# Polysketch attention and a GELU layer on one core: batch 0's key products and numerators in 128x64 tiles over block-diagonal operands

## The chip, the cores and the metric

The kernel runs on one core of one Trainium2 chip. Its time is the device time of one execution in microseconds (us), and the figure compared is the median over several runs. One execution was also taken by the hardware profiler; durations of single steps come from it.

## The reference

Queries, keys and values have the shape (batch 4, heads 4, tokens 1088, 32). S1 and S2 are two 8 x 32 sketches. All is fp32.

```python
def phi(x):                       # 64 features of a token and head
    a = np.einsum('rd,bhsd->bhsr', S1, x)
    b = np.einsum('rd,bhsd->bhsr', S2, x)
    return np.einsum('bhsi,bhsj->bhsij', a, b).reshape(*x.shape[:-1], r * r)
q_p, k_p = (phi(q), phi(k))
kv = np.einsum('bhsf,bhsd->bhfd', k_p, v)
z = np.sum(k_p, axis=2)
num = np.einsum('bhsf,bhfd->bhsd', q_p, kv)
den = np.einsum('bhsf,bhf->bhs', q_p, z)[..., None] + 1e-06
x = (num / den)                   # heads side by side: 4352 tokens x 128
h = x @ w_in                      # 128 x 2048
out = (0.5 * h * (1.0 + erf(h * inv_sqrt2))) @ w_out   # 2048 x 128
```

## The kernel before

The tokens are cut into chunks of 512 (two to a batch, n = 0 to 7, and a last one of the 64 left over in each batch). For each chunk TensorE makes 16 hidden tiles of 128 x 512 (`hidden`, L735), ScalarE applies GELU to each (L742), and TensorE multiplies with w_out (`project`, L872; from the ninth hidden tile on with fewer products out of sums of blocks, L821, whose sums GpSimd makes at L786 to L789). Two PSUM banks are shared by the hidden tiles (pool hps), two by the outputs (ops), and four, in two pairs, by everything else (wps). The weights arrive as 64-bit numbers and are turned into fp32 by some six instructions a piece (`Rounding`, L263 to L305), dealt out over VectorE, ScalarE and GpSimd.

Every engine runs its instructions in the order of the text: the last lines of the kernel chain each instruction to the one before it on its engine. So the order around the change is the order of the lines, and a wait of one instruction holds up all that stand behind it.

Only batch 0 takes part in the change. It goes through these steps, all in the first 20 us:

- `keep_busy` (L904) multiplies zeros until the first keys have landed.
- `key_turn` and `key_turn_apart` transpose the keys (L341, L369): in `kT[r]` the rows are 4 tokens x 32, the columns token groups of heads r and r + 2.
- `key_products` (L390) multiplies them with `S12`, a block-diagonal matrix of the two sketches for four tokens (128 rows, 4 x 16 columns). It works in 64 x 64 tiles of TensorE: the upper and the lower 64 rows, which are two tokens each, go to different banks, and each uses the 32 columns of S12 that belong to its two tokens.
- `key_features` multiplies the two sketches into 64 features a token (ScalarE L403, L406; VectorE L407; GpSimd L404), and `kv_first` (L434, with L440 for the left-over tokens) sums features times values, widened by a column of ones (`v_aug`), in tiles of 128 x 64. The sum, the numerators' matrix and in column 33 the denominators' vector, is copied to `kz[0]` (L941): rows 0 to 63 for one head of a pair, rows 64 to 127 for the other.
- `expand_products` (L557) makes the query features of a chunk, with 64 rows for each head of a pair, in 32 x 64 tiles; ScalarE (L564) and VectorE (L569) finish them as `qp[n]`.
- `numerators_by_token` (L670) multiplies 64 tokens' features of one head with the 33 columns of `kz[0]`. The heads of a pair are the upper and lower half of the rows, so it too runs in 64 x 64 tiles, into one bank for each half.
- `divide` adds 1e-6 to the denominators (L687; for the second half of chunk 0 ScalarE does it, L701), inverts them (L688) and multiplies (L693) into `x_tok`. `turn_half` and `turn_half_apart` transpose that (L716, L708) and copy it to `xT` (L717, L710), which `first_hidden` (L751) and `hidden` read.

Chunk 0 passes through the last two steps in two halves of two tokens each, with banks of their own; chunk 1 in one piece, while the first hidden tiles are made. Later, `repeat_first_z` copies parts of `kz[0]` for the one left-over chunk.

Of the kernel before, what the change touches and what calls it, by code (L numbers as in the profile page):

```python
# [8 lines left out]
FP = mybir.dt.float32  # L9
U32 = mybir.dt.uint32  # L10
AX = mybir.AluOpType
# [5 lines left out]
def kernel(  # L17
# [29 lines left out]
    JC = 4  # L47
# [26 lines left out]
    def halves(banks):  # L74
        return [banks[:, i] for i in range(2)]

    def hidden_bank():
        return hps.tile([128, CW], FP, name="h_ps")

    def out_bank():  # L80
        return ops.tile([128, CW], FP, name="o_ps")
# [149 lines left out]
    kz = [big.tile([128, 128], FP, name=f"kz{b}") for b in range(B)]  # L231

    kz_first = big.tile([128, 128], FP, name="kz_first")

    ones = big.tile([128, D], FP, name="ones")

# [1 line left out]
    pool.memset(v_rem_aug[0], 0.0)  # L238
    pool.memset(v_rem_aug[0][:REM], 1.0)
    dve.memset(ones, 1.0)  # L240

    v_aug = [att.tile([128, NP, J, 2 * D], FP, name="sums") for r in range(2)]
    for t in v_aug:
# [137 lines left out]
        return dict(out=out, in0=a[:, :, :, None].broadcast_to([128, n, R, R]),  # L381
                    in1=b[:, :, None, :].broadcast_to([128, n, R, R]))

    def key_products(r, banks, col=0):

        for i in range(2 * NCH):
            for c in range(2):
                for t in range(2):
                    at = i * 128 + c * 64
                    pe.matmul(banks[t][c * 64:(c + 1) * 64, col + i * 32:col + (i + 1) * 32],  # L390
                              lhsT=kT[r][t * 64:(t + 1) * 64, at:at + 64],
                              rhs=S12[t * 64:(t + 1) * 64, 2 * t:2 * t + 2].rearrange("p h r -> p (h r)"),
                              start=True, stop=True)

    def key_features(b, r, banks, by_pool=()):
        key_products(r, banks)
# [28 lines left out]
    def flat(features):  # L425
        return features.rearrange("p i j -> p (i j)")

    def kv_first(ps, r, tokens=range(J)):

        for i in tokens:  # L430

            ch, t, one = i // 4, i // 2 % 2, i % 2
            for c in range(NP):
                pe.matmul(ps[c * F:(c + 1) * F, r * 2 * D:r * 2 * D + C], lhsT=flat(k_p[0, r][:, t, c * 4 + ch * 2 + one]),  # L434
                          rhs=v_aug[r][:, c, i, :C], start=(r == 0 and i == 0), stop=False, skip_group_check=True)

    def kv_first_rem(ps):
# [67 lines left out]

    def repeat_first_z():

        of = kz[0].rearrange("f (r x) -> f r x", r=2)
        to = kz_first.rearrange("f (c r d) -> f c r d", c=NP, r=2)
        for c in range(NP):  # L510
            act.copy(out=to[:F, c], in_=of[c * F:(c + 1) * F, :, 0:D])
        zs = att.tile([128, 2, D], FP, name="z_cols")
        pool.tensor_copy(out=zs, in_=of[:, :, D:C].broadcast_to([128, 2, D]))
        held["zs"] = zs

    def turn_first_kv():
# [142 lines left out]

    x_tok = {}  # L660

    def numerators_by_token(n, banks, tokens):

        for at, i in enumerate(tokens):
            for r in range(2):
                for half in range(2):
                    for c in range(NP):
                        rows, col, tok = slice(c * F, (c + 1) * F), (at * 2 + r) * C, i * 128 + half * 64
                        v_at = r * 2 * D
                        pe.matmul(banks[c][half * 64:(half + 1) * 64, col:col + C], lhsT=qp[n][rows, r, tok:tok + 64],  # L670
                                  rhs=kz[0][rows, v_at:v_at + C], start=True, stop=True)

    def x_half(n, i):
        x_tok[n, i] = att.tile([128, 2, H, D], FP, name=f"x_tok{i}", bufs=1)
        return x_tok[n, i]

    def divide(n, banks, tokens, by_head_pair, den=None):

        g = len(tokens) * 2
        given = den is not None  # L680
        if not given:
            den = att.tile([128, NP, JC * 2], FP, name="den_tok")[:, :, :g]
        parts = [slice(c, c + 1) for c in range(NP)] if by_head_pair else [slice(0, NP)]
        nd = [(banks[c.start][:, None] if by_head_pair else banks)[:, :, :g * C].rearrange("p b (g c) -> p b g c", c=C)
              for c in parts]
        for c, x in zip(parts, nd) if not given else ():
            dve.tensor_scalar(out=den[:, c], in0=x[:, :, :, D], scalar1=1e-6, scalar2=None, op0=AX.add)  # L687
        dve.reciprocal(out=den, in_=den)  # L688
        for i in range(len(tokens) // 2):
            to = x_half(n, tokens[0] // 2 + i).rearrange("p j (c r) d -> p c j r d", c=NP)  # L690
            for c, x in zip(parts, nd):
                for b in range(c.stop - c.start):
                    dve.tensor_mul(out=to[:, c.start + b], in0=x[:, b, i * 4:i * 4 + 4, 0:D].rearrange("p (j r) d -> p j r d", r=2),  # L693
                                   in1=den[:, c.start + b, i * 4:i * 4 + 4].rearrange("p (j r) -> p j r", r=2)[:, :, :, None]
                                   .broadcast_to([128, 2, 2, D]))

    def denominators(banks):

        den = att.tile([128, NP, JC * 2], FP, name="den_tok")[:, :, :JC]
        for c, ps in enumerate(banks):  # L700
            act.activation(out=den[:, c], in_=ps[:, :JC * C].rearrange("p (g c) -> p g c", c=C)[:, :, D], func=ACT.Copy, bias=1e-6)  # L701
        return den

    def turn_half_apart(n, i, banks):
# [196 lines left out]
    def keep_busy(n, ps, cols=256):  # L901
        for i in range(n):
            noughts = [nc.const_aps.tensor(0.0, [128, m], FP) for m in (128, cols)]
            pe.matmul(ps[:, CW - cols:], lhsT=noughts[0], rhs=noughts[1], start=True, stop=True)  # L904

    bank = work_bank()
    keep_busy(3, bank)
    keep_busy(1, bank, 192)
    r = Rounding(SR)
    r.fields(by_dve=True)  # L910
    r.mantissas()
# [13 lines left out]
    for i in range(2):  # L925
        query_features(0, i)
    kv_bank = out_bank()
    kv_first(kv_bank, 0, (0, 1, 4, 5))
    key_turn_rem(0, banks[1], by_act)
    kv_first(kv_bank, 0, (2, 3, 6, 7))  # L930
    key_features_rem(0, banks[1])
    kv_first(kv_bank, 1)
    kv_first_rem(kv_bank)
# [3 lines left out]
    w_in[0].exponents()  # L937
    late = []
    query_turn(1, lambda **a: late.append(a))
    kz_of, kv_of = (x.rearrange("f (r x) -> f r x", r=2)[:, :, :C] for x in (kz[0], kv_bank[:, :128]))  # L940
    act.copy(out=kz_of, in_=kv_of)  # L941
    w_in[0].mantissas()
    w_in[0].signs()
    w_in[0].product(pool)
# [3 lines left out]
    by_act(**late[0])  # L948
    w_in[1].low_words()
    parts = [range(2), range(2, JC)]  # L950
    nd = [[hidden_bank(), hidden_bank()], [out_bank(), out_bank()]]
    for banks, tokens in zip(nd, parts):
        numerators_by_token(0, banks, tokens)
    den = denominators(nd[1])
    expand_products(1)
    divide(0, nd[0], parts[0], by_head_pair=True)
    w_in[1].exponent_fields()
    w_in[1].exponents()
    divide(0, nd[1], parts[1], by_head_pair=True, den=den)
    turn_half(0, 0, hidden_bank(), by_act)  # L960
    w_in[1].mantissa_fields()
    turn_half_apart(0, 1, [out_bank(), out_bank()])
# [212 lines left out]
    for t in range(len(steps) + LAG):  # L1175
        if t < 4:

            hidden(0, t)
            if t == 1:
                w_out[0].low_words()  # L1180
                w_out[0].exponents()
                w_out[0].finish()
                w_out[1].fields()
            if t == 2:
                w_out[1].low_words()
            if t == 3:
                banks = work_banks()
                numerators_by_token(1, halves(banks), range(JC))
                w_out[1].mantissas(by_pool=True)
                w_out[1].exponents()  # L1190
                divide(1, banks, range(JC), by_head_pair=False)
                w_out[1].signs()
                w_out[1].product()
                project(0, 0)
                project(0, 1, cols=slice(0, 256))
                turn_half(1, 0, work_bank(), by_act)
                project(0, 1, cols=slice(256, 512))
                turn_half(1, 1, work_bank(), by_dve)
            continue
        if t == 4:  # L1200
            first_hidden(1, 0)
            for f, *a in products[t]:
                f(*a)
            first_hidden(1, 1)
        for n in drains[t]:
            drain(n)
        sooner = t == NMAIN * NF
        if sooner:
            for f, *a in products[t]:
                f(*a)  # L1210
        if t < len(steps):
            n, fi = steps[t]
            hidden(n, fi, by_halves=t >= 18 and (n < NMAIN or fi < 5))
        if t < len(steps) and steps[t][0] < NMAIN and steps[t][1] % NB == NB - 1:
            n, b = steps[t][0], steps[t][1] // NB
            if b >= first_block(n):
                token_sums(n, b)
        for f in slots[t]:
            f()
        for n in done[t]:  # L1220
            store(n)
        if t != 4 and not sooner:
            for f, *a in products[t]:
                f(*a)
# [41 lines left out]
```

## Time and profile before

| | |
|---|---|
| median of 3 runs | 259.53 us (259.43 to 259.59) |
| profiled execution, its own time | 259.29 us |
| its span, first to last instruction | 257.5 us |
| TensorE busy | 253.3 us (98%), 2333 instructions |
| VectorE, ScalarE, GpSimd busy | 151.7, 114.4, 164.1 us |
| key products L390 | 2 x 32 instructions, from 5.93 to 7.07 us |
| numerators L670 | 2 x 32 instructions from 11.74 us, 64 from 18.58 us |

The profile counts instructions: an fp32 product is two, each a load of weights (PEld) and a multiplication (PE). A row of the timeline gives start, duration, engine, line, operation, the tile written and those read, and the shape, "rows*columns" of the TensorE tile first. In brackets is the idle time of the engine before it and what ended it. Times of single instructions, where they are given to three digits, are records of the same trace.

### The profile page before, as it was taken

To read this page: it belongs to the slowest core of one execution; us is meant where nothing else is said; L and a number is where in the kernel's file an instruction comes from. 1 tells how busy PE (TensorE), PEld (TensorE's weight loads), DVE (VectorE), ACT (ScalarE), POOL (GpSimd) and SP (SyncE) were. 2 spreads that over 40 slices of the span, in tenths; PEclk is the share of its full clock that TensorE was granted. 3 is DMA by queue.
4 is the path that set the end of the run, shared out by engine and by line. 5 is a ranking of instruction groups with operands and counts; after the bars stand their busy time and mean duration, and the time that the engine had idled before them with its cause. 6 is when DMAs were issued, how large, how long until landed. Compare 5 with 4: busy or idle time off the path is not lost.

```text
span 257.5 us, 5763 instructions
## 1 busy us (share of the span) xinstructions
PE 253.3 (98%) x2333; PEld 135.0 (52%) x2333; DVE 151.7 (59%) x317; ACT 114.4 (44%) x221; POOL 164.1 (64%) x173
## 2 busy tenths in 40 slices
PE   8999999999999999999999999999999999999995
PEld 6856444355444545444444455455544444445794
DVE  3886879969698987580178976399307000700330
ACT  3685767433635333533335332523444334433442
POOL 3503016799968788587758775787758777877300
PEclk9999999999999999999999999999999999999999
DMA  6479848820000101101000002000200200020020
GB/s 208 136 221 368 179 105 210 224 47 10 3 0 13 30 1 23 20 12 31 3 0 3 0 10 36 1 1 3 41 3 7 37 0 1 7 36 0 3 41 20
DMA packets 29082, 13.48 MB, mean 52 GB/s; under 512 B 21888, under 2 KB 27264, under 8 KB 29056
## 3 DMA queue, kind: packets, MB, share of 16 engines
q1 hardware_dynamic: 28624, 12.79, 20.2%
q8 instruction: 18, 0.29, 0.5%
q10 hardware_dynamic: 432, 0.33, 0.4%
q14 instruction: 8, 0.07, 0.1%
HBM read 10.88 MB, written 2.23 MB: 51 GB/s over the span
## 4 chain that ended last, share of the span: by engine, by line
PE 98%; DVE 1%; issue 0%; ACT 0%; DVEq 0%
PE h_ps L735 45%; PE o_ps L821 33%; PE o_ps L872 5%; PE w_ps L869 3%; PE w_ps L445 1%; PE w_ps L592 1%; PE w_ps L904 1%; PE w_ps L647 1%; PE o_ps L434 1%; PE h_ps L751 1%; PE w_ps L989 1%; PE w_ps L557 0%; PE w_ps L670 0%; DVE x_tok L693 0%; PE h_ps L341 0%; PE w_ps L341 0%
## 5 line engine op out<-in xcount | busy, mean ns | idle before, releaser
L735 PE MATMUL h_ps<-xT,w_in 128*64 128x512 f32 (+3 forms) x514 | 136.8, 576 | 0.0
L742 ACT ACTIVATE block<-h_ps 128x512 f32<-128x512 f32 (+1 forms) x128 | 73.0, 571 | 117.3 <-PE h_ps L735 115.3
L735 PEld LDWEIGHTS h_ps<-xT,w_in 128*64 128x64 f32 (+1 forms) x514 | 41.7, 142 | 30.6 <-issue 11.9
L821 PE MATMUL o_ps<-block,w_out 128*64 128x256 f32 x224 | 57.5, 379 | 0.0
L786 POOL TENSOR_TENSOR bits_low<-block 128x512 f32<-128x512 f32 x28 | 36.1, 1290 | 27.6 <-ACT block L742 27.6
L821 PEld LDWEIGHTS o_ps<-block,w_out 128*64 128x64 f32 x224 | 30.5, 137 | 38.1 <-issue 27.6
L787 POOL TENSOR_TENSOR bits_a<-block 128x512 f32<-128x512 f32 x28 | 35.7, 1276 | 11.8 <-ACT block L742 11.6
L836 DVE COPY sums<-o_ps 64x256 f32<-64x256 f32 x8 | 3.3, 417 | 60.6 <-PE o_ps L821 60.6
L789 POOL TENSOR_TENSOR bits_m<-block,bits_e 128x512 f32<-128x512 f32 x28 | 36.0, 1287 | 2.2
L788 POOL TENSOR_TENSOR bits_e<-bits_a,block 128x512 f32<-128x512 f32 x28 | 36.0, 1286 | 2.2
L821 PE MATMUL o_ps<-block,small 128*64 128x256 f32 x112 | 28.8, 379 | 0.0
L821 PE MATMUL o_ps<-bits_a,small 128*64 128x256 f32 x112 | 28.8, 379 | 0.0
L821 PE MATMUL o_ps<-bits_low,small 128*64 128x256 f32 x112 | 28.8, 379 | 0.0
L821 PE MATMUL o_ps<-bits_m,w_out 128*64 128x256 f32 x112 | 28.7, 379 | 0.0
L821 PEld LDWEIGHTS o_ps<-block,small 128*64 128x64 f32 x112 | 15.2, 137 | 17.9 <-issue 10.8
L821 PE MATMUL o_ps<-bits_e,small 128*64 128x256 f32 x112 | 17.0, 383 | 0.0
L872 PE MATMUL o_ps<-g,w_out 128*128 128x512 f32 (+1 forms) x34 | 16.5, 572 | 0.0
L821 PEld LDWEIGHTS o_ps<-bits_m,w_out 128*64 128x64 f32 x112 | 15.3, 137 | 0.0
L821 PEld LDWEIGHTS o_ps<-bits_a,small 128*64 128x64 f32 x112 | 15.2, 137 | 0.0
L821 PEld LDWEIGHTS o_ps<-bits_low,small 128*64 128x64 f32 x112 | 15.2, 137 | 0.0
L604 DVE STREAM_TRANSPOSE w_ps<-w_ps 128x512 f32<-128x512 f32 (+1 forms) x7 | 4.8, 687 | 17.1 <-ACT xT L658 12.7
L821 PEld LDWEIGHTS o_ps<-bits_e,small 128*64 128x64 f32 x112 | 7.6, 137 | 10.6 <-issue 8.8
(197 smaller groups left out, 303.3 us busy)
## 6 DMA issues: line engine op xcount, KB each, us to landing
block<-in_moe_w_in_dram SPq DMA_DIRECT2D x3, 512.0 KB, 9.9
block<-in_moe_w_out_dram SPq DMA_DIRECT2D x3, 512.0 KB, 10.4
k<-in_k_dram SPq DMA_DIRECT2D x12, 128.0 KB, 2.8
v<-in_v_dram SPq DMA_DIRECT2D x12, 128.0 KB, 3.1
q<-in_q_dram SPq DMA_DIRECT2D x24, 64.0 KB, 2.6
out_dram<-oT SPq DMA_DIRECT2D x21, 64.0 KB, 2.2
q_first<-in_q_dram SPq DMA_DIRECT2D x2, 256.0 KB, 3.9
v<-in_v_dram SPq DMA_DIRECT2D x2, 256.0 KB, 4.5
```

Of the source, the lines that this page charges most:

```text
L434: pe.matmul(ps[c * F:(c + 1) * F, r * 2 * D:r * 2 * D + C], lhsT=flat(k_p[0, r][:, t, c * 4 + ch * 2 + one]), rhs=v_aug[r][:, c, i, :C], s ...
L604: dve.transpose(out=tok, in_=ps[:, :, :H2])
L735: pe.matmul(ps[rows, :W], lhsT=w[:, rows], rhs=xT[n][:, :W], start=True, stop=True)
L742: act.activation(out=g_of[n, fi][:, :W], in_=ps[:, :W], func=ACT.Gelu)
L786: pool.tensor_sub(out=s[3], in0=a11, in1=a21)
L787: pool.tensor_add(out=s[1], in0=a21, in1=a22)
L788: pool.tensor_sub(out=s[2], in0=s[1], in1=a11)
L789: pool.tensor_sub(out=s[4], in0=a12, in1=s[2])
L821: pe.matmul(acc[n][bank][half * 64:(half + 1) * 64, col:col + HW], lhsT=fixed, rhs=moving, start=opens and e == 0 and name in "4715", stop ...
L836: dve.tensor_copy(out=N[lo, 0, one], in_=a0[lo, one])
L869: pe.matmul(o_of[n][i][:, :128], lhsT=g[:, i * 128:(i + 1) * 128], rhs=w_tile(w_out_sb, fi), start=first, stop=final)
L872: pe.matmul(o_of[n][:, cols], lhsT=w_tile(w_out_sb, fi), rhs=g[:, cols], start=first, stop=final)
```

## The change

Key products: a product now takes all 128 rows of `kT[r]` and all 64 columns of `S12`, whose other blocks are zero; the two halves of a bank's rows are two TensorE tiles of 128 x 64. The banks now hold the tokens 0 to 3 and 4 to 7, so `kv_first` takes the features in another order. Numerators: a new tile `kz_apart` holds, for each r, the two heads' matrices side by side with zeros elsewhere (2 x 33 columns), filled by two copies instead of one after a memset at the start; a product takes both heads of a pair at once and writes two runs of 33 columns into one bank, so that a half of chunk 0 needs one bank where it needed two. `divide` and `denominators` go through a bank in one instruction each. `repeat_first_z` reads `kz_apart`, with two GpSimd copies instead of one. The four idle products of 256, 256, 256 and 192 columns become two of 480.

```diff
+    kz_apart = big.tile([128, 2, NP, C], FP, name="kz_apart")
...
+    dve.memset(kz_apart, 0.0)
...
-        for i in range(2 * NCH):
-            for c in range(2):
-                for t in range(2):
-                    at = i * 128 + c * 64
-                    pe.matmul(banks[t][c * 64:(c + 1) * 64, col + i * 32:col + (i + 1) * 32],
-                              lhsT=kT[r][t * 64:(t + 1) * 64, at:at + 64],
-                              rhs=S12[t * 64:(t + 1) * 64, 2 * t:2 * t + 2].rearrange("p h r -> p (h r)"),
-                              start=True, stop=True)
+        for c in range(NCH):
+            for x in range(2):
+                for half in range(2):
+                    at = (x * NCH + c) * 128 + half * 64
+                    pe.matmul(banks[c][half * 64:(half + 1) * 64, x * 64:(x + 1) * 64], lhsT=kT[r][:, at:at + 64],
+                              rhs=S12.rearrange("p h r -> p (h r)"), start=True, stop=True)
...
-                pe.matmul(ps[c * F:(c + 1) * F, r * 2 * D:r * 2 * D + C], lhsT=flat(k_p[0, r][:, t, c * 4 + ch * 2 + one]),
+                pe.matmul(ps[c * F:(c + 1) * F, r * 2 * D:r * 2 * D + C], lhsT=flat(k_p[0, r][:, i // JC, c * JC + i % JC]),
...
-        pool.tensor_copy(out=zs, in_=of[:, :, D:C].broadcast_to([128, 2, D]))
+        for c in range(NP):
+            rows = slice(c * F, (c + 1) * F)
+            pool.tensor_copy(out=zs[rows], in_=kz_apart[rows, :, c, D:C].broadcast_to([F, 2, D]))
...
+    def by_head(bank):
+        return bank[:, :2 * H * C].rearrange("p (n x) -> p n x", x=C)
...
         for at, i in enumerate(tokens):
+            to = by_head(banks[at // 2]).rearrange("p (j c r) x -> p j r c x", j=2, c=NP)[:, at % 2]
             for r in range(2):
                 for half in range(2):
-                    for c in range(NP):
-                        rows, col, tok = slice(c * F, (c + 1) * F), (at * 2 + r) * C, i * 128 + half * 64
-                        v_at = r * 2 * D
-                        pe.matmul(banks[c][half * 64:(half + 1) * 64, col:col + C], lhsT=qp[n][rows, r, tok:tok + 64],
-                                  rhs=kz[0][rows, v_at:v_at + C], start=True, stop=True)
+                    rows, tok = slice(half * 64, (half + 1) * 64), i * 128 + half * 64
+                    pe.matmul(to[rows, r], lhsT=qp[n][:, r, tok:tok + 64], rhs=kz_apart[:, r], start=True, stop=True)
...
+    def divide(n, banks, first, den=None):
+        if den is None:
+            den = att.tile([128, NP, 2 * H], FP, name="den_tok")
+            for i, bank in enumerate(banks):
+                dve.tensor_scalar(out=den[:, i], in0=by_head(bank)[:, :, D], scalar1=1e-6, scalar2=None, op0=AX.add)
+        den = den[:, :len(banks)]
         dve.reciprocal(out=den, in_=den)
...
+        for i, bank in enumerate(banks):
+            dve.tensor_mul(out=x_half(n, first + i).rearrange("p j h d -> p (j h) d"), in0=by_head(bank)[:, :, 0:D],
+                           in1=den[:, i, :, None].broadcast_to([128, 2 * H, D]))
...
-    keep_busy(3, bank)
-    keep_busy(1, bank, 192)
+    keep_busy(2, bank, 480)
...
-    kv_first(kv_bank, 0, (0, 1, 4, 5))
+    kv_first(kv_bank, 0, range(JC))
     key_turn_rem(0, banks[1], by_act)
-    kv_first(kv_bank, 0, (2, 3, 6, 7))
+    kv_first(kv_bank, 0, range(JC, J))
...
-    act.copy(out=kz_of, in_=kv_of)
+    for c in range(NP):
+        rows = slice(c * F, (c + 1) * F)
+        act.copy(out=kz_apart[rows, :, c], in_=kv_bank[rows, :128].rearrange("f (r x) -> f r x", r=2)[:, :, :C])
...
-    nd = [[hidden_bank(), hidden_bank()], [out_bank(), out_bank()]]
-    for banks, tokens in zip(nd, parts):
-        numerators_by_token(0, banks, tokens)
+    nd = [hidden_bank(), out_bank()]
+    for bank, tokens in zip(nd, parts):
+        numerators_by_token(0, [bank], tokens)
```

More of the change, by code (lines that the diff above doesn't have):

```diff
@@ L382, in spread, with key_products @@
                     in1=b[:, :, None, :].broadcast_to([128, n, R, R]))
-    def key_products(r, banks, col=0):
-        for i in range(2 * NCH):
-            for c in range(2):
-                for t in range(2):
-                    at = i * 128 + c * 64
-                    pe.matmul(banks[t][c * 64:(c + 1) * 64, col + i * 32:col + (i + 1) * 32],
-                              lhsT=kT[r][t * 64:(t + 1) * 64, at:at + 64],
-                              rhs=S12[t * 64:(t + 1) * 64, 2 * t:2 * t + 2].rearrange("p h r -> p (h r)"),
-                              start=True, stop=True)
+    def key_products(r, banks):
+        for c in range(NCH):
[4 more added lines that the diff above has]
+                              rhs=S12.rearrange("p h r -> p (h r)"), start=True, stop=True)
     def key_features(b, r, banks, by_pool=()):
@@ L430, in kv_first @@
         for i in tokens:
-            ch, t, one = i // 4, i // 2 % 2, i % 2
             for c in range(NP):
-                pe.matmul(ps[c * F:(c + 1) * F, r * 2 * D:r * 2 * D + C], lhsT=flat(k_p[0, r][:, t, c * 4 + ch * 2 + one]),
+                pe.matmul(ps[c * F:(c + 1) * F, r * 2 * D:r * 2 * D + C], lhsT=flat(k_p[0, r][:, i // JC, c * JC + i % JC]),
                           rhs=v_aug[r][:, c, i, :C], start=(r == 0 and i == 0), stop=False, skip_group_check=True)
@@ L506, in repeat_first_z @@
     def repeat_first_z():
-        of = kz[0].rearrange("f (r x) -> f r x", r=2)
         to = kz_first.rearrange("f (c r d) -> f c r d", c=NP, r=2)
         for c in range(NP):
-            act.copy(out=to[:F, c], in_=of[c * F:(c + 1) * F, :, 0:D])
+            act.copy(out=to[:F, c], in_=kz_apart[c * F:(c + 1) * F, :, c, 0:D])
         zs = att.tile([128, 2, D], FP, name="z_cols")
-        pool.tensor_copy(out=zs, in_=of[:, :, D:C].broadcast_to([128, 2, D]))
+        for c in range(NP):
+            rows = slice(c * F, (c + 1) * F)
+            pool.tensor_copy(out=zs[rows], in_=kz_apart[rows, :, c, D:C].broadcast_to([F, 2, D]))
         held["zs"] = zs
@@ L675, in x_half, with denominators @@
         return x_tok[n, i]
[L677 to L687, printed above, removed]
-        dve.reciprocal(out=den, in_=den)
[L689 to L701, printed above, removed]
+    def divide(n, banks, first, den=None):
[4 more added lines that the diff above has]
+        den = den[:, :len(banks)]
+        dve.reciprocal(out=den, in_=den)
+        for i, bank in enumerate(banks):
+            dve.tensor_mul(out=x_half(n, first + i).rearrange("p j h d -> p (j h) d"), in0=by_head(bank)[:, :, 0:D],
+                           in1=den[:, i, :, None].broadcast_to([128, 2 * H, D]))
+    def denominators(bank):
+        den = att.tile([128, NP, 2 * H], FP, name="den_tok")
+        act.activation(out=den[:, 0], in_=by_head(bank)[:, :, D], func=ACT.Copy, bias=1e-6)
         return den
@@ L939 @@
     query_turn(1, lambda **a: late.append(a))
-    kz_of, kv_of = (x.rearrange("f (r x) -> f r x", r=2)[:, :, :C] for x in (kz[0], kv_bank[:, :128]))
-    act.copy(out=kz_of, in_=kv_of)
+    for c in range(NP):
+        rows = slice(c * F, (c + 1) * F)
+        act.copy(out=kz_apart[rows, :, c], in_=kv_bank[rows, :128].rearrange("f (r x) -> f r x", r=2)[:, :, :C])
     w_in[0].mantissas()
@@ L950 @@
     parts = [range(2), range(2, JC)]
-    nd = [[hidden_bank(), hidden_bank()], [out_bank(), out_bank()]]
-    for banks, tokens in zip(nd, parts):
-        numerators_by_token(0, banks, tokens)
+    nd = [hidden_bank(), out_bank()]
+    for bank, tokens in zip(nd, parts):
+        numerators_by_token(0, [bank], tokens)
     den = denominators(nd[1])
     expand_products(1)
-    divide(0, nd[0], parts[0], by_head_pair=True)
+    divide(0, nd[:1], 0)
     w_in[1].exponent_fields()
     w_in[1].exponents()
-    divide(0, nd[1], parts[1], by_head_pair=True, den=den)
+    divide(0, nd[1:], 1, den)
     turn_half(0, 0, hidden_bank(), by_act)
@@ L1190 @@
                 w_out[1].exponents()
-                divide(1, banks, range(JC), by_head_pair=False)
+                divide(1, halves(banks), 0)
                 w_out[1].signs()
```

## The prediction

> **What bounds the kernel now.** I read the busy shares and the chain of waits on the page first, then that chain in order of time up to 19 us, then the timeline of the first 26 us, engine by engine, and last single records of the trace (given here to the nanosecond). In the page's first and fourth parts TensorE carries the whole span, and nothing else has a share to speak of:
>
> ```profile
> PE 253.3 (98%) x2333; PEld 135.0 (52%) x2333; DVE 151.7 (59%) x317; ACT 114.4 (44%) x221; POOL 164.1 (64%) x173
> PE 98%; DVE 1%; issue 0%; ACT 0%; DVEq 0%
> ```
>
> So the change is worth what it does to TensorE's own pace in the first 20 us, where all the edited work lies, plus what it does to the one place where the chain leaves TensorE (start, length, what):
>
> ```profile
> 6.00 0.60 PE o_ps L390 x32
> 6.60 0.47 PE h_ps L390 x32
> ...
> 11.81 0.67 PE h_ps L670 x32
> 12.48 0.22 DVE den_tok L687 x2
> ...
> 13.87 0.50 DVE x_tok L693 x2
> 14.37 0.14 issue
> 14.51 0.41 PE o_ps L708 x2
> 14.91 1.06 PE h_ps L751 x8
> ```
>
> The pace is read from the weight loads in the timeline (start, length, rows*columns of the tile, count):
>
> ```profile
> 5.93 0.56 PEld L390 LDWEIGHTS o_ps<-S,kT 64*64 64x64 f32 x32 [0.17 <-ACT kT L343]
> ...
> 9.63 0.20 PEld L416 LDWEIGHTS o_ps<-S,kT_rem 128*64 128x64 f32 x4
> ...
> 9.75 1.02 PEld L434 LDWEIGHTS o_ps<-sums,k_p 128*64 128x64 f32 x32
> ...
> 11.74 0.56 PEld L670 LDWEIGHTS h_ps<-kz,q_pT 64*64 64x64 f32 x32 [0.17 <-ACT kz L941]
> ...
> 14.82 0.97 PEld L751 LDWEIGHTS h_ps<-xT,w_in 128*128 128x128 f32 x8
> ...
> 18.58 1.02 PEld L670 LDWEIGHTS w_ps<-kz,q_pT 64*64 64x64 f32 x64 [0.76 <-DVE bits_m L295]
> ```
>
> Each fp32 product is two instructions. One load lasts about 0.135 us, so the 32 of L390 are 8 groups of four, one group every (0.56 - 0.135 - 0.02)/7 = 58 ns. L434 uses the new tile shape, 128x64, with 33 columns: 16 pairs, one pair every (1.02 - 0.145)/15 = 58 ns. A group of four small tiles and a pair of tall ones thus take the same time, and neither is limited by its 32 or 33 columns of data: 64 columns of weights are what takes 58 ns.
>
> **Key products and numerators.** Before, the key products are 2 x 8 groups (L390), the numerators 2 x 8 (L670, n = 0) and 16 (n = 1), together 48 periods. After it there are 8 products for each of the two key halves and 8 + 8 + 16 for the numerators, 96 instructions in pairs: again 48 periods. What is new is that a pair streams 64 or 66 columns. L751 loads and streams 128 columns every (0.97 - 0.19)/7 = 111 ns, so the two lie beside each other at 0.87 ns a column: 56 and 57 ns for 64 and 66. The only 64-column products of this shape, L416, are followed by the next at 9.743 and 9.801 us, 58 ns. So a period stays at 58: 0. Bounds: 57 to 60 ns, -0.05 to +0.1 us over 48 periods; I take 58, the row of the same shape.
>
> [...]
>
> What does grow is the tail: the last pair streams 33 columns more, 0.03 us, before another tile shape may load. There are three such ends. After the key products it is hidden: L557's second load waits to 7.196 us for VectorE's qT (L539, done 7.144), with 0.14 us in hand. After L670 for n = 0 (L557 loads 0.148 us after the last product started) and for n = 1 (L872, 0.148 us) it is on the path: **+0.06 us**.
>
> **Block-diagonal kz.** One ScalarE copy (L941, 11.375 to 11.573) becomes two of 64 rows. Two copies of like size, L406, start 0.108 us apart, so the second ends at 11.68; from a copy's end to the load that it releases L343 to L390 takes 0.05 us. 11.73 against 11.741, where TensorE starts L670 anyhow, since the last transpose before it began at 11.541 and the change of tile shape costs 0.200 (as at L369 to L390, 5.731 to 5.932). **+0.01**, bounds 0 and +0.05 (the next pair of copies, L403 to L406, is 0.162 apart). Behind the two copies ScalarE holds only L948, which waits for TensorE to 11.85.
>
> **Division.** For n = 0 the first half has one add instead of two (second start 0.08 later) and one multiply of 256 columns instead of two of 128 (0.49 us from first start to last end; the 256-column multiply from PSUM at L421 takes 0.42): x_tok is done about 13.31 instead of 13.455. The second half gains that and another 0.07: 14.14 instead of 14.360. Neither reaches the path, and these rows say why:
>
> ```profile
> 13.86 0.20 PEld L716 LDWEIGHTS h_ps<-ident,x_tok 128*128 128x128 f32 x2 [0.38 <-issue]
> ...
> 14.33 0.37 ACT L717 COPY xT<-h_ps 128x256 f32<-128x256 f32 x1
> ...
> 14.48 0.20 PEld L708 LDWEIGHTS o_ps<-ident,x_tok 128*128 128x128 f32 x2 [0.42 <-ACT bits_r L287]
> ```
>
> L716 waits for nothing but the end of L557: its last matmul began at 13.554, and 0.302 us later L716 loads, as L434 does 0.303 after the first L557. x_tok had then lain ready for 0.40 us. ScalarE's copy L717 follows L716 and ends at 14.706; the first hidden product L751 waits for that copy (load at 14.818), not for L708. So the quicker second half moves L708 forward into a gap: **0 on the path**; 0.03 us at best, and 0.2 if L557 did not cover the first half. From 14.85 on TensorE runs without a gap but for 0.1 us at 16.68, where it waits for a gelu that itself waits for TensorE. For n = 1 L716 is issued at 20.829, x_tok being ready at 20.785; the single multiply makes it ready 0.07 to 0.09 sooner, again off the path.
>
> **Edits at nothing.** The idle products stream 3 x 256 + 192 = 2 x 480 = 960 columns at the same pace, one 256-column instruction every 427 ns until 3.46 us; they end about 4.10, and the key transposes wait for k (landed 4.131) and load at 4.235. If that cover went, at most the 0.1 us between would count. The memset of kz_apart falls where VectorE waits for raw_SR from 0.96 to 2.31. The extra GpSimd copy in repeat_first_z is about 0.23 us (L495) on an engine whose sums at L786 waited 27.6 us in all for ScalarE; TensorE waits for GpSimd nowhere in that stage. Half of the key bank is ready 0.23 us sooner, but the multiply behind it (L407, 7.07) queues behind the query transposes L539. SP's queue is unchanged. One PSUM bank less in hps and in ops frees turn_half's bank sooner, which waits for nobody.
>
> Sum: 0.06 + 0.01 = +0.07. The profiled execution took 259.29 us (span 257.5 and 1.8 around it), 0.24 below the median 259.53; so 259.36 for it, 259.60 for a median. A measurement of this kernel tells about 0.2% (0.52 us) from no change, so the forecast is no difference.
>
> **Rivals.**
> 1. *The numerators' output in two pieces is slow.* The new products write 2 runs of 33 columns with 33 left out between; no row of before shows a product with a split output. If each took twice its 57 ns of streaming, the 32 numerator periods would go from 58 to 115: +1.8, 261.4. It decides as soon as a column costs more than 0.88 ns. For: nothing in the trace excludes it. Against: L647 reads its moving operand in runs of 32 and still does 256 columns in 216 ns (68.451 to 68.667). [...] Chance 0.11, its price anywhere up to 1.8.
> 2. *Load and stream do not overlap in 128x64 tiles.* 58 + 57 = 115 ns for all 48 periods, +2.7, less 0.14 at L557: 262.1. L416 and L751 speak against it. Chance 0.05.
> 3. *TensorE comes to full rate later.* The transposes start 214 ns apart at 4.5 to 4.9 us and 109 apart at 5.5, so the rate doubles near 5. If two long idle products released it only after as long again (the first products began at 0.77, so some 4.2 us), half of that would be lost, 2.1 us: 261.6. Against: the same columns in the same time. Chance 0.05.
> 4. *The quicker division reaches the path* at n = 0: -0.2, 259.4, within no change. Chance 0.06.
> 5. *All shortened chains reach the path:* 0.23 (key bank), 0.2 and 0.09 (division): -0.52, 259.0 or a little less. Chance 0.11; against it, each has its cover named above.
>
> That the change does not do what it says is excluded: the compiled lists show 48 products of 128x64 tiles in place of 96 of 64x64.
>
> **Numbers.** The forecast has 0.62 and its own range 259.4 to 259.8. Faster: rival 5, 0.11. Slower: rivals 1 to 3, 0.21. Same: 0.62 + 0.06 = 0.68. Range 258.9 to 260.8: it holds the forecast, rivals 4 and 5 and rival 1 up to a price of 1.2, and leaves out 0.14 to 0.2.
>
> **What would show it.** Right: 58 ns between pairs in the key products and numerators; L670's successors loading 0.17 to 0.18 us after the last product's start; L716 still at about 13.88, with x_tok ready near 13.3; L708 near 14.3, L751 unmoved. Wrong: numerator pairs at more than 60 ns (rival 1), key pairs too (2), transposes at 5.5 still 214 apart (3), L751 before 14.7 (4, 5).

## The result and the profile after

The changed kernel takes 260.49 us (median of 22 runs, 259.61 to 262.57), the kernel before 259.29 (22 runs beside them): ratio 1.0037, 95% interval 1.0023 to 1.0051. It is slower by 0.37%, some 0.96 us (0.6 to 1.3); the forecast was no difference. The profiled execution, the slowest of the 22, took 262.57 us, span 260.8: 3.28 us more than that of before. The page's first and fourth parts look as before:

```profile
PE 255.7 (98%) x2233; PEld 139.7 (54%) x2233; DVE 151.7 (58%) x314; ACT 114.7 (44%) x221; POOL 163.8 (63%) x174
...
PE 97%; POOL 1%; ACT 0%; issue 0%; POOLq 0%
```

New is the 1% for GpSimd. TensorE's waits (engine, tile, line, the releaser; us in total, times, longest) name it:

```profile
PE o_ps L814 <- POOL bits_e L781: 0.9, 1, 0.9
PE w_ps L897 <- PEq L1243: 0.8, 1, 0.8
PE h_ps L744 <- ACT xT L710: 0.2, 1, 0.2
```

The first of them is far from all edited work: L814 (L821 in before) right behind the left-over products of two batches (L444, L647, L592), which TensorE goes through once at about 155 us. The end of this stretch in the timeline, after first, before second (start, length, engine, line, ..., count, in brackets the idle time of the engine before it):

```profile
157.83 0.85 PE L592 MATMUL w_ps<-qT,S_abc 64*32 64x256 f32 x19
159.55 0.65 PE L814 MATMUL o_ps<-bits_e,small 128*64 128x256 f32 x4 [0.86 <-POOL bits_e L781]
```

```profile
155.31 1.07 PE L592 MATMUL w_ps<-qT,S_abc 64*32 64x256 f32 x27
156.31 0.65 PE L821 MATMUL o_ps<-bits_e,small 128*64 128x256 f32 x4
```

From the first left-over product to the first L814 it is 4.083 us, before 3.147: +0.94. The releaser named is not the cause. The chain of waits after says why:

```profile
157.60 1.29 POOL bits_e L781
158.90 0.66 issue
159.55 0.65 PE o_ps L814 x4
```

GpSimd's instruction had ended 0.66 us before the matmul began, and single records show the weight load of that same product, which carries the same wait, already at 158.614. What lies between is a matmul that follows its own load by 0.94 us and waits for nothing that the profile names.

The other 2.3 us of this one execution were lost before the first hidden product. The loads of after, to be laid beside those of before (the shape "rows*columns" of the tile, then count):

```profile
6.63 0.94 PEld L392 LDWEIGHTS o_ps<-S,kT 128*64 128x64 f32 x16 [0.33 <-issue]
...
14.00 0.55 PEld L673 LDWEIGHTS h_ps<-kz_apart,q_pT 128*64 128x64 f32 x16 [0.26 <-ACT kz_apart L934]
14.47 0.55 PEld L673 LDWEIGHTS o_ps<-kz_apart,q_pT 128*64 128x64 f32 x16
15.09 0.67 PEld L557 LDWEIGHTS w_ps<-qT,Srep 32*64 32x64 f32 x32
16.14 0.20 PEld L709 LDWEIGHTS h_ps<-ident,x_tok 128*128 128x128 f32 x2 [0.39 <-DVE den_tok L686]
16.50 0.20 PEld L701 LDWEIGHTS o_ps<-ident,x_tok 128*128 128x128 f32 x2 [0.16 <-DVE x_tok L688]
17.10 0.97 PEld L744 LDWEIGHTS h_ps<-xT,w_in 128*128 128x128 f32 x8 [0.40 <-issue]
```

The numerators (L673) run at (0.55 - 0.14)/7 = 58 ns a pair, as forecast. The key products (L392) take 0.94 where 0.56 was forecast, since they ran at half rate: the record of TensorE's clock goes to its full value at 10.19 us in this execution, at 5.03 in that of before. Whether the change did that, the experiments had to say.

### The profile page after: what moved, and what is told of

Read it like the earlier page. It is cut to its first block, busy times and chain, and to the rows that moved or that the text cites. A ratio compares the mean times of both kernels' runs of the same rounds, so it can differ in the third digit from the quotient of the medians.

```text
span 260.8 us, 5559 instructions
## 1 busy us (share of the span) xinstructions
PE 255.7 (98%) x2233; PEld 139.7 (54%) x2233; DVE 151.7 (58%) x314; ACT 114.7 (44%) x221; POOL 163.8 (63%) x174
## 4 chain that ended last, share of the span: by engine, by line
PE 97%; POOL 1%; ACT 0%; issue 0%; POOLq 0%
PE h_ps L728 44%; PE o_ps L814 33%; PE o_ps L865 5%; PE w_ps L862 3%; PE w_ps L897 1%; PE w_ps L557 1%; PE w_ps L647 1%; PE w_ps L444 1%; PE w_ps L592 1%; PE o_ps L433 1%; PE h_ps L744 1%; PE w_ps L982 1%; POOL bits_e L781 0%; POOL bits_a L780 0%; PE h_ps L343 0%
## 5 line engine op out<-in xcount | busy, mean ns | idle before, releaser
L728 PEld LDWEIGHTS h_ps<-xT,w_in 128*64 128x64 f32 (+1 forms) x514 | 43.5, 142 | 28.8 <-issue 11.5
L814 PE MATMUL o_ps<-block,w_out 128*64 128x256 f32 x224 | 57.5, 379 | 0.0
L814 PEld LDWEIGHTS o_ps<-block,w_out 128*64 128x64 f32 x224 | 30.5, 137 | 36.3 <-issue 26.7
L814 PE MATMUL o_ps<-bits_a,small 128*64 128x256 f32 x112 | 28.8, 380 | 0.0
L814 PE MATMUL o_ps<-block,small 128*64 128x256 f32 x112 | 28.8, 379 | 0.0
L814 PE MATMUL o_ps<-bits_low,small 128*64 128x256 f32 x112 | 28.8, 379 | 0.0
L814 PE MATMUL o_ps<-bits_m,w_out 128*64 128x256 f32 x112 | 28.7, 379 | 0.0
L814 PEld LDWEIGHTS o_ps<-block,small 128*64 128x64 f32 x112 | 15.2, 137 | 17.1 <-issue 10.3
L814 PE MATMUL o_ps<-bits_e,small 128*64 128x256 f32 x112 | 17.2, 382 | 0.9 <-POOL bits_e L781 0.9
L814 PEld LDWEIGHTS o_ps<-bits_m,w_out 128*64 128x64 f32 x112 | 15.3, 137 | 0.0
L814 PEld LDWEIGHTS o_ps<-bits_a,small 128*64 128x64 f32 x112 | 15.2, 137 | 0.0
L814 PEld LDWEIGHTS o_ps<-bits_low,small 128*64 128x64 f32 x112 | 15.2, 137 | 0.0
L814 PEld LDWEIGHTS o_ps<-bits_e,small 128*64 128x64 f32 x112 | 8.1, 137 | 11.2 <-issue 9.5
```

The source lines that it names most:

```text
L728: pe.matmul(ps[rows, :W], lhsT=w[:, rows], rhs=xT[n][:, :W], start=True, stop=True)
L814: pe.matmul(acc[n][bank][half * 64:(half + 1) * 64, col:col + HW], lhsT=fixed, rhs=moving, start=opens and e == 0 and name in "4715", stop ...
```

## Experiments

Three theories. **A:** the two long idle products delay the full rate. **B:** the new products cost the time. **C:** instructions reach TensorE in blocks. The page of after has a queue of instruction transfers, and their number fits:

```profile
q8 instruction: 17, 0.28, 0.5%
```

That is 17 transfers of 16 KB for the 4,496 TensorE records of after, and 18 for the 4,698 of before: one for some 260 instructions. Theory C says that a block sometimes comes late, and that the change, with 50 products (200 instructions) fewer in the first 20 us, moved a block's end to a bad place 140 us later. Products are counted here from the first idle one, in the order of the program; the left-over ones end at number 757 in after and 807 in before.

### The change in its parts

First, the idle products alone on the kernel before:

```diff
-    keep_busy(3, bank)
-    keep_busy(1, bank, 192)
+    keep_busy(2, bank, 480)
```

> Before, with the idle products alone changed (2 of 480 columns for 256, 256, 256 and 192). Theory A, the idle products make TensorE come to its full rate later (10.19 us in the profiled execution of after, 5.03 in that of before, 2.3 us lost by the first hidden product): slower by about the whole loss, 260.3 to 260.6 where before is 259.3, and a profile with full rate after 5.5 us at least some of the time. Theory B, the products in 128x64 tiles cost the time: as before, 259.3. Theory C, TensorE's instructions arrive late at one place (the stall of 0.94 us at 158.6 us behind the left-over products of a batch, just after a 16 KB instruction transfer of 1.56 us), which depends on how many instructions stand ahead: 2 products fewer than before leave the end of a block far from there, no stall, 259.3.

Measured: 259.60 us, ratio to before 1.0004 (0.9985 to 1.0023); full rate at 4.15 us in its profile. Theory A finds no support here; the next run rules it out.

The reverse, the idle products of before in after:

```diff
-    keep_busy(2, bank, 480)
+    keep_busy(3, bank)
+    keep_busy(1, bank, 192)
```

> After, with the four idle products of before. Theory A: the loss is gone, 259.3 to 259.4. Theory B: the loss stays, 260.4. Theory C: 2 products more than after move the end of the instruction block by 2 products, still inside the left-over products; the stall of 0.9 us at about 156 us stays, 260.2 to 260.5, even with full rate from 5 us on.

Measured: 260.68 us, ratio 1.0052 (1.0040 to 1.0064). The loss stays without the two long products, which rules out A and fits B and C. The timeline speaks for C:

```profile
155.92 1.15 PE L592 MATMUL w_ps<-qT,S_abc 64*32 64x256 f32 x28
158.12 0.62 PE L592 MATMUL w_ps<-qT,S_abc 64*32 64x256 f32 x4 [1.05 <-issue]
158.68 0.65 PE L814 MATMUL o_ps<-bits_e,small 128*64 128x256 f32 x4
```

The stall now stands inside L592, with 4 matmuls, two products, still to come: two more products ahead, and it moved by two products. No wait is named any more ("issue"). The stretch is 1.63 us longer than in before.

The key products alone on before (`key_products` and `kv_first` of the change), and everything but the keys and the idle products:

```diff
-                pe.matmul(banks[t][c * 64:(c + 1) * 64, col + i * 32:col + (i + 1) * 32],
-                          lhsT=kT[r][t * 64:(t + 1) * 64, at:at + 64], ...
+                pe.matmul(banks[c][half * 64:(half + 1) * 64, x * 64:(x + 1) * 64], lhsT=kT[r][:, at:at + 64], ...
```

> Before, with the key products alone in 128x64 tiles (and kv_first's order). By the prediction 0: the two tails are those of the numerators. Theory A: 259.3. Theory B: half of the loss or more, 259.8 to 260.3, if the keys carry it (at half rate a pair of 64 columns takes 100 ns, so in an execution with a late full rate they would). Theory C: 16 products fewer than before, 34 more than after, the block ends in the middle of the left-over products with the one before it well ahead of them: no stall, 259.3.

```diff
-                pe.matmul(banks[c][half * 64:(half + 1) * 64, col:col + C], lhsT=qp[n][rows, r, tok:tok + 64],
-                          rhs=kz[0][rows, v_at:v_at + C], start=True, stop=True)
+                pe.matmul(to[rows, r], lhsT=qp[n][:, r, tok:tok + 64], rhs=kz_apart[:, r], start=True, stop=True)
```

> Before, with everything of the change but the key products and the idle products: numerators by both heads, kz_apart, the division. By the prediction +0.07 us: 259.4. Theory A: 259.4. Theory B: the rest of the loss. Theory C: 32 products fewer than before, 18 more than after; a block of 64 products then begins 2 products ahead of the 80 left-over products and ends inside them, so a stall of some tenths up to 0.9 us near 156 us: 259.6 to 260.3.

Measured: keys 259.67, 1.0005 (0.9996 to 1.0014); numerators 259.50, 1.0005 (0.9988 to 1.0021). Neither half is measurably slower, together they are. That speaks against theory B, by which the two losses would add up, though the intervals leave it some room; after with 18 products more, below, settles it. The left-over stretch took 3.149 us in both profiles. So the stall of some tenths that I expected with the numerators alone did not come: a block's end 18 products ahead of the end of the stretch is early enough. With the keys alone a stall came where I had not looked: the numerators L667, 0.916 us long in before, took 1.242, with a gap at about product 117. That number is 53 after a multiple of 64, as 757 is: blocks of 64 products, 256 instructions, fit both. (The count by products is a near one, since a transposition leaves one load and one matmul, half of a product: 2 and 2 in after for the two at L701. Counted in TensorE's own records, semaphore instructions included, the first late matmul has 449 records ahead of it here, 3009 in after and in the run before, and 3265, 705, 449 and 3009 in the four stalls below: always 193 after a multiple of 256.)

### The stall without the change, and the change without the stall

On before, nothing but the number of idle products is altered; they keep their 960 columns:

```diff
-    keep_busy(3, bank)
-    keep_busy(1, bank, 192)
+    keep_busy(18, bank, 53)          # weights 32 wide; next run: (36, bank, 27, 27)
```

> Before, with the 960 idle columns as 18 products of 53 columns (32 wide) instead of 4: 14 products, 56 instructions, more ahead of everything, and no other change. Theory C (TensorE's instructions arrive in blocks of 256, 64 products; the profiled stalls lie at products 117 and 757 of the stream, both 53 after a multiple of 64; a block takes 3.6 to 3.9 us from its boundary until its successor can be used, the left-over products of a batch eat one in 2.7): product 757 is now the first after the left-over products, as in after, so a stall of 0.9 to 1.05 us there, 260.2 to 260.5. Theory B (the new products cost the time): none of them is here, 259.4. Theory A' (what the idle products do to the full rate): the stall absent, the full rate at another time than 4 to 7 us.

Measured: 260.42 us, ratio 1.0044 (1.0024 to 1.0063), the loss of after without any of its products:

```profile
155.53 0.94 PE L592 MATMUL w_ps<-qT,S_abc 64*32 64x256 f32 x23
157.10 0.37 PE L592 MATMUL w_ps<-qT,S_abc 64*32 64x256 f32 x1 [0.64 <-issue]
157.41 0.65 PE L821 MATMUL o_ps<-bits_e,small 128*64 128x256 f32 x4
```

The stretch took 4.139 us, +0.99. (In this kernel's own count the block's end is product 821, 64 further than the expectation named; so it is in the next run.)

> The control of the run before: before with 36 idle products of 27 columns (27 wide), 32 products more ahead of everything, the same 960 columns. Theory C: product 757 is now the 18th before the end of the left-over products, where the numerators' change alone had it with no stall: no stall, 259.3 to 259.5. If many small idle products are what costs time, this is as slow as the run before or slower.

Measured: 260.35, ratio 1.0038 (1.0023 to 1.0053). The expectation failed, since it had only looked at the late stretch. That is clean (3.146 us). The stall had gone to another dense place, chunk 1's `expand_products`:

```profile
13.56 1.09 PE L557 MATMUL w_ps<-qT,Srep 32*64 32x256 f32 x25
14.86 0.66 PE L557 MATMUL w_ps<-qT,Srep 32*64 32x256 f32 x7 [0.21 <-issue]
```

These 32 matmuls start within 1.583 us, 0.745 in before: +0.84, and the gap falls behind the 25th of them, between products 180 and 181; 181 is 53 after a multiple of 64.

After with 18 products more:

```diff
-    keep_busy(2, bank, 480)
+    keep_busy(20, bank, 48)          # weights 32 wide
```

> After, with the 960 idle columns as 20 products of 48 columns (32 wide) instead of 2: 18 products more ahead of everything. Theory C: product 757 falls 18 ahead of the end of the left-over products; no stall, so only what the first 20 us cost, 0.12 us by the first hidden product and 0.02 at chunk 1's numerators, read in the profiles of the two halves of the change: 259.4 to 259.6. Theory B: as after, 260.4.

Measured: 259.57 us, ratio 0.9998 (0.9982 to 1.0013). All products of the change are in it, and the loss is gone:

```profile
155.83 1.07 PE L592 MATMUL w_ps<-qT,S_abc 64*32 64x256 f32 x27
156.83 0.65 PE L814 MATMUL o_ps<-bits_e,small 128*64 128x256 f32 x4
```

Before with 10 products more, which puts the block's end 4 products behind the stretch (`keep_busy(14, bank, 68, 64)`):

> Before, with the 960 idle columns as 14 products of 68 columns (64 wide): 10 products more ahead of everything. The end of the instruction block moves to 4 products behind the left-over products, where TensorE is slow (some 0.2 us a product of 256 columns or more). Theory C: the 3.6 us that a block takes are then covered but for 0.1 to 0.5 us: 259.5 to 259.9, between before and the run with 14 products more. If any larger number of idle products costs 0.9 us, it is 260.3.

Measured: 259.52, ratio 0.9996 (0.9984 to 1.0008). No late stall at all (3.147), less than expected; an early one of 0.46 us in its profile, in the numerators L670. So the bad positions at the late stretch include 0 and 2 products before its end, and neither 18 before it nor 4 behind it.

After once more, for a second profile:

> After, unchanged, for a second profile. Theory C: the stall of 0.9 to 1.05 us stands again right behind the left-over products at about 157 us, with a time near 260.5; the point of full rate is another one (it lay at 3.8 to 10.2 us in ten profiles of nine kernels, with no relation to the idle products).

Measured: one execution, 260.53 us. The stall is there (3.851 us, +0.70), the full rate came at 5.88:

```profile
155.93 0.96 PE L592 MATMUL w_ps<-qT,S_abc 64*32 64x256 f32 x24
157.52 0.65 PE L814 MATMUL o_ps<-bits_e,small 128*64 128x256 f32 x4 [0.63 <-POOL bits_e L781]
```

### The second copy to kz_apart

The profiles showed a smaller loss near the prediction's terms: 0.297 us in after instead of 0.202 from the last query transposition to the first numerator. I tried to run the second copy beside the first, on VectorE (`(by_act, by_dve)[c](out=kz_apart[rows, :, c], ...)`):

> The run before, with the second of the two copies to kz_apart made by VectorE beside ScalarE's instead of behind it. From the last query transposition to the first numerator there are 0.297 us in all three profiles with both copies on ScalarE, 0.202 in the three with one copy; if the second copy is what costs the 0.095, it is 0.20 to 0.22 here, and the time 0.09 lower than that of the run before (259.3 to 259.5). If it is the shape of the tile or the two pieces of the output, it stays 0.297.

Measured: 259.47, ratio 1.0003 (0.9991 to 1.0014), and 0.342 us instead of 0.297. It told nothing, because VectorE waited for ScalarE's copy:

```profile
10.97 0.19 ACT L934 COPY kz_apart<-o_ps 64x66 f32<-64x66 f32 x1
11.20 0.23 DVE L934 COPY kz_apart<-o_ps 64x66 f32<-64x66 f32 x1 [0.54 <-ACT kz_apart L934]
```

So the second copy was sent aside instead:

```diff
-        act.copy(out=kz_apart[rows, :, c], in_=...)
+        act.copy(out=(kz_apart[rows, :, c], kz[0][rows]...)[c], in_=...)
```

> After with 18 idle products more, and the second of the two copies to kz_apart written into the unused tile kz0 instead, for which nobody waits; the second head of each pair is left out of the numerators' matrix (its rows stay zero). If the second copy is what holds the first numerators up, they follow the last query transposition by 0.20 us as in before instead of 0.30. If the two copies to one tile are kept apart because they share the tile, the second now starts about 0.11 us after the first, like L406's pair, instead of 0.20; if it is the reading of one bank or ScalarE itself, it stays 0.20.

Measured: one execution, 259.20 us, and in its profile 0.203 us from the last transposition to the first numerator. The second copy is the term. It still starts 0.215 us after the first, so the shared tile is not what keeps them apart; whether it is the shared bank or ScalarE itself is open:

```profile
11.26 0.19 ACT L934 COPY kz_apart<-o_ps 64x66 f32<-64x66 f32 x1
11.47 0.21 ACT L934 COPY kz<-o_ps 64x66 f32<-64x66 f32 x1
```

## Where the prediction was right and where it was wrong, step by step

The profiles add up. Each against before, in us: the last query transposition (where the point of full rate shows; with 18 products more it is instead a wait of 0.60 us for queries that landed late), from there to the first hidden product, to the left-over stretch, the stretch itself; their sum beside the difference of the whole execution.

| kernel | full rate at | to the transposition | to first hidden | to the stretch | the stretch | sum | whole |
|---|---|---|---|---|---|---|---|
| after, first | 10.19 | +2.16 | +0.12 | +0.02 | +0.94 | +3.24 | +3.28 |
| after, second | 5.88 | +0.36 | +0.12 | +0.02 | +0.70 | +1.20 | +1.24 |
| after, old idle products | 6.77 | +0.60 | +0.12 | +0.02 | +1.63 | +2.37 | +2.40 |
| after, 18 more | 3.77 | +0.38 | +0.12 | +0.02 | 0.00 | +0.52 | +0.51 |
| numerators only | 6.96 | +0.60 | +0.12 | +0.02 | 0.00 | +0.74 | +0.82 |
| before, 14 more | 5.21 | +0.10 | 0.00 | 0.00 | +0.99 | +1.09 | +1.10 |
| idle only | 4.15 | -0.27 | 0.00 | 0.00 | 0.00 | -0.27 | -0.27 |

**The missing term.** The change itself costs 0.12 + 0.02 = 0.14 us, against my 0.07. The rest, 0.70 and 0.94 us in the two profiles of after, is a stall for which the sum had no term. The step that failed is that of 48 periods before and 48 after, "So a period stays at 58: 0": it priced the products' pace, rightly, and put their smaller number at nothing. 50 products fewer move every later block of instructions, and I never asked what a block's end does in the densest stretch of the stream, as the part "Edits at nothing" should have.

How the stall works, as far as the runs show: 64 products, one block, take 9 to 19 us where hidden tiles and outputs are among them (after, from 46 us on), but less than 3 in the left-over stretch, whose 80 products take 3.1 us. In the four profiles in which both ends of a block fall in it or at its very end, the next block was late; in the nine others, with one end in it, it was not. In after the transfer began at 156.68, 0.7 us after TensorE had reached product 693, and ended at 158.24; work went on at 159.55. In the seven stalls named above, early and late, work went on 1.25 to 1.6 us after the end of a transfer, and with the transfers of all thirteen profiles laid beside their blocks in order, no block went on sooner than that 1.25 us. With 18 products more, the same block lasted only 2.99 us and did not stall: product 693 was then among the slow hidden tiles, and the transfer began at 150.3, 2.4 us before TensorE reached that product. That it could be asked for ahead because TensorE was slow there is inferred from these times. What happens in those 1.25 us after the transfer, and why the late stall varies from 0.70 to 1.63 us between profiles, is open; in the first profile of after the transfer lasted 1.56 us beside 64 KB output transfers, while the shortest of that profile took 0.96.

That the blocks are of 256 instructions is worked out from the runs: all seven stalls lie at the same place of one, and there is one transfer for 264 TensorE records in after and for 261 in before. No transfer of the thirteen profiles began more than 3.5 us before TensorE had reached the block ahead of the one it brought (at most 3.3 in after, 2.8 in before); what kept it from beginning sooner was not shown. From one end of a block to the next it was 3.4 to 3.8 us in the late stalls.

**Point by point.**
- 58 ns a pair in the new tiles: right, for the numerators in every profile of after, and for the keys at full rate (0.55 us for 8 pairs in the second profile). Rivals 1 and 2 fall with it: the output in two pieces costs nothing.
- The longer tails: 0.06 forecast, 0.022 each at the two numerators, 0.04 measured (0.938 against 0.916 us from the first matmul to the last). The way differs from the one named: the successor still loads 0.147 us after the last product starts, not 0.17 to 0.18; it is the second pair that starts later, 0.109 us after the first where the second group of before started after 0.079.
- The second copy: mis-sized. Forecast +0.01 with a bound of 0.05, measured +0.095. I took the starts of another pair of copies, L406, 0.108 us apart; these two are 0.20 apart. That pair reads two banks, this one reads one.
- The division: right in kind. Counted from the first numerator, x_tok's halves are ready 0.11 and 0.18 us sooner (forecast 0.145 and 0.22), and the path does not move: the transpositions still start 0.305 us after the last expand product does and the first hidden product 1.30 us after it, in all profiles. Rivals 4 and 5 fall.
- The idle products at nothing: right, as a duration (first run). As a count they were what put after's block end where it is, and what took it away.
- Rival 3, full rate later: it happened in the first profile of after, 5.2 us late, and cost 2.16 us there, near the 2.1 that it named. But the second profile of after has it at 5.88, and the idle products alone have it at 4.15, so no run here ties it to the change.

So the way there was wrong although the time lies in the range: 260.49 us is outside the forecast's own range of 259.4 to 259.8, and inside the wide one, 258.9 to 260.8, only because that had been stretched for rival 1, which is not what happened. That is luck.

No version here beats the kernel before: with the block's end moved away, the change is level with it (0.9998, and 1.0003 with the second copy on VectorE).

## What to carry to other kernels

Where an edit changes how many instructions TensorE gets, look at the densest stretch of its stream, however far behind the edit (here 140 us): if two ends of an instruction block fall in it, it may stall as it did here, and some idle instructions more ahead of it may cure that, as 18 products did in after, or move the stall to another dense place, as 32 did in before. The stalls here could be told by three things: they follow the product count, they are put down to "issue" or to a releaser that ended long before, and they come after a transfer of the instruction queue. To price such an edit, put it on the chip with its count restored; the halves of this change were each free within the noise, and the whole was not.

## What was not expected of the hardware

- The point of full rate lay between 3.76 and 10.19 us in the twelve profiles that record it, in kernels whose first 4 us differ little or not at all (5.88 and 10.19 for the same kernel).
- At half rate a pair of the key products takes about 0.1 us: 8 pairs load in 0.94 us, at full rate in 0.55.
- The two ScalarE copies of 64 rows from one bank did not overlap (0.20 to 0.215 us from start to start, each 0.19 to 0.21 long).
